# First four weight units converted during attention, and the odd groups' high part on GpSimd

## Chip, core and metric

The kernel runs on one core of a Trainium2 chip. The metric is the device time of one execution in microseconds, from the first to the last work of the core; lower is better.

## What is computed

An attention with head mixing (2 batches, 12 heads, 448 positions, head size 64) feeds two feed-forward blocks over 896 tokens of width 768. All inputs are float32 and the weights of the blocks are read as float64.

```python
scores = scale * q @ k.T                      # per head, then mixed over heads by w_pre
scores = scores - max(scores)
attn = exp(scores); attn = attn / (sum(attn) + 1e-9)
attn = mixed over heads by w_post;  x = attn @ v
xn = x / sqrt(mean(x*x) + 1e-6) * rms_g       # first block, width 1536
x = (silu(xn @ w_gate) * (xn @ w_val)) @ w_out
h = x @ w_in                                  # second block, width 2048
out = where(h > 0, h, exp(min(h, 0)) - 1) @ w_out2
```

## The kernel before

Products are made in split precision: each operand is a high part (float16 or a rounded float32) and a low part (the rest), and three matmuls add high x high, high x low, low x high (`gemm`, L202 to L204).

**Weights.** They come as *units* of 128 x 768 (one 768 KB load into a `raw` buffer, L208). A unit of the first block is *small* and is converted in eight stages: `rebase` (ScalarE L229, VectorE L232), `sign` (VectorE L237, L245), `join` (VectorE L251, for the second of a pair also L270), then once a pair `bound` (a TensorE matmul, L277) and `factor` (VectorE L284 to L290), then `scaled` (six ScalarE activations, L301), `high16` (ScalarE L305) and `low16` (VectorE L309). The result is a `whl` buffer, of which there are three. Units 0 and 2 are gate weights, 1 and 3 value weights of the same 128 columns.

**Attention.** It is cut into 90 groups (45 a batch) of 10 query positions x 12 heads = 120 rows. A hand-written loop over steps t = -6 to 94 records for each step one piece of the pipeline for several groups: the scores of a later group's rows come from `hq` (TensorE L469, copied by ScalarE L487, written to memory and read again as `sg`); the split of odd or even groups at t+3 (`g_split`: ScalarE L536, GpSimd L537, even groups alone); `g_premix` at t+1 (TensorE L544 for odd, *whole* groups, L547 to L549 for even ones); `g_max` at t (VectorE L556); `g_exp` at t (ScalarE L564); `g_sum` and `g_recip` at t-1 (VectorE L572, L579); `g_high` at t-1 (eh, VectorE L595, or ScalarE L593 for 20 of the 45 odd groups, in steps 20 to 43 and from 74); `g_low` at t-2 (el, VectorE L602); `g_postmix` at t-3 (TensorE L623, 12 matmuls); `g_out` at t-4 (ScalarE L635). Each engine does its instructions in the order in which they are recorded.

**Windows.** After every six or seven groups a window of tokens goes on: attention times v (TensorE L659), then a chain of stages, one a step: `squares` (VectorE L665, GpSimd L672 to L675 or, for the last two, ScalarE L670), `mean` (TensorE L681), `root` (VectorE L688, GpSimd L692: rstd), `diagonal` (VectorE L696: dg), `spread` (TensorE L702), `normed` (VectorE L705), `high` (ScalarE L711) and `low` (VectorE L714) of x. The first gate matmuls of the first block (`first_gate`) fill TensorE between these at the end; they need units 0 and 1, and from 292.58 us on the last window's x too.

**Where the conversions stand.** A list `tail` holds the pieces of units 0 and 1, one a step, which are begun when the list of scores `hq` is empty; a list `more` holds those of units 2 and 3, one for each piece of filling at the end. The high and low parts of q and k (`par`) live in nine rooms of their own and, the rest of them, in `whl` and `raw` buffers, which the weights can't use meanwhile.

Of the kernel before, what the change touches and what calls it, by code (L numbers as in the profile page):

```python
# [22 lines left out]
def block_kernel(  # L23
# [15 lines left out]
    nc = tc.nc  # L39
# [72 lines left out]
    g_top = const.tile([P, P], BF16, name="g_top")  # L112
    m1f = const.tile([GP, GP], F32, name="m1f")
    m1h = const.tile([GP, GP], F32R, name="m1h")
    m1l = const.tile([GP, GP], F32R, name="m1l")
    m2h = const.tile([GP, H, GI], F16, name="m2h")
# [9 lines left out]

    def mixing():

# [85 lines left out]
    def convert(u):  # L214
# [40 lines left out]
        def high():  # L255
            st["p"] = whl = wpool.tile([P, 2, n], F32R, tag="whl", name="whl", bufs=3)
            nc.scalar.activation(out=whl[:, 0], in_=st["w"], func=ACTF.Copy)  # L257
# [45 lines left out]
        def high16():  # L303
            st["p"] = whl = wpool.tile([P, 2, n], F16, tag="whl", name="whl16", bufs=3, padded_shape=[P, 4, n])
            nc.scalar.activation(out=whl[:, 0], in_=st["w"], func=ACTF.Copy)  # L305
# [64 lines left out]
    def attention(actx):  # L370
# [60 lines left out]
        def parts_of(b, p, tag):  # L431

            i = 2 * p + (tag == "qt")
            if (b, i) not in par:
                own = ["par"] * 9 + ["whl"] * 3 if b == 0 else ["raw"] * 2 + ["par"] * 9 + ["whl"]
                if own[i] == "par":
                    t = ap.tile([P, 2, S], F32R, tag="par", name="par", bufs=9)
                else:
                    n = 3 if own[i] == "whl" else 2
                    t = wpool.tile([P, 2 * KD * P], F32R, tag=own[i], name="par_" + own[i][0], bufs=n)  # L440
                    t = t[:, :2 * S].rearrange("p (t s) -> p t s", t=2)
                par[b, i] = t
            return [par[b, i][:, j] for j in range(2)]
# [137 lines left out]

        TURNS, LAST = range(20, 44), 74

        def high_on_act(b, g):
            i = b * NG + g
            return whole(b, g) and (i in TURNS or i >= LAST)

        def g_high(b, g):
            r = rows_of(g) * H
            e32, rs = ex[b, g]  # L590
            eh = ap.tile([GP, S], F16, tag="eh", name="eh", bufs=4)
            if high_on_act(b, g):
                nc.scalar.activation(out=eh[:r], in_=e32[:r], func=ACTF.Copy, scale=rs[:r])  # L593
            else:
                nc.vector.tensor_scalar_mul(eh[:r], e32[:r], rs[:r])  # L595
            ex[b, g].append(eh)
# [151 lines left out]
        MIX = 3  # L748
        mix = mixing()
        load_first()  # L750
# [48 lines left out]

        EARLY_GATES, GAP, FILL, END = 2, 2, 1, 1  # L800
        conv_now = []
# [15 lines left out]
        tail = [lambda: load_to(2)] + [lambda: None] * 2  # L817
        tail += unit() + [lambda: load_to(3)] + unit() + [lambda: load_to(4)] + scaling() + scaling()
        more = unit() + [lambda: load_to(5)] + unit() + [lambda: load_to(6)] + scaling()

        gates = []

        def fill(k):
            if not gates and not first_ps:
                while tail:
                    tail.pop(0)()
                for j in range(EARLY_GATES):
                    gates.extend(first_gate(j))
# [80 lines left out]
    def run(u, mm, stages):  # L909

        load_to(begun[0] + 2)
        v = begun[0]
        conv = []
        rest = next_scaled(u + 3 if u == 0 else u + 2)
        if v < len(units) and v <= u + (4 if units[v][4] else 2):
            conv = next_convert()
        conv = conv + [None] * (5 - len(conv))
        stages = stages + [None] * (4 - len(stages))

        def go(*fs):  # L920
# [13 lines left out]
        return out
# [190 lines left out]
```

## Time and profile before

| | before |
|---|---|
| median of 3 runs (us) | 782.35 (781.74 to 783.04) |
| profiled execution (us) | 782.59 |
| its span (us) | 780.9 |
| TensorE busy | 747.8 us, 96% |
| VectorE busy | 552.1 us, 71% |
| ScalarE busy | 438.5 us, 56% |
| GpSimd busy | 94.6 us, 12% |

The span runs from the first to the last instruction. A busy TensorE is one with a matmul under way, so holes are what is left of a stretch; TensorE's clock has two levels, 1.2 and 2.4 GHz, and a granted clock of 1.00 is the higher. Attention ends at about 293 us; the two blocks follow.

### The profile page before, as it was taken

How to read it: one execution, taken by the hardware profiler on the slowest of the kernel's cores; microseconds unless marked ns; L12 is line 12 of the kernel's file. 1: busy time of each engine (PE TensorE's matmuls, PEld its weight loads, DVE VectorE, ACT ScalarE, POOL GpSimd, SP SyncE). 2: the span in 40 equal slices, each digit the busy share in tenths (PEclk: the TensorE clock that was granted, in tenths of full speed). 3: DMA queues.
4: the chain of work that ended last, by engine and by line, in shares of the span. 5: the costliest groups of instructions: out<-in, count | busy, mean ns of one | idle time of the engine just before them, and what ended most of it. 6: DMA issues, size and time to landing. Idle time of an engine off the chain costs nothing.

```text
span 780.9 us, 14563 instructions
## 1 busy us (share of the span) xinstructions
PE 747.8 (96%) x5683; PEld 590.3 (76%) x5683; DVE 552.1 (71%) x1101; ACT 438.5 (56%) x910; POOL 94.6 (12%) x117
## 2 busy tenths in 40 slices
PE   7789999999998879999999999999999999999996
PEld 5446787777776654555555589999999999999996
DVE  4358997788899867878878766653888788643731
ACT  3478788878777845666576622322776665221310
POOL 0122344334445300000000000000000000000000
PEclk8689999999999999999999999999999999999999
DMA  8698965668675023333333223322444244442602
GB/s 186 202 298 263 188 142 147 186 177 251 188 200 156 3 84 122 99 112 114 122 122 119 83 83 122 122 81 72 131 122 119 87 119 120 124 121 79 174 22 71
DMA packets 92873, 104.05 MB, mean 133 GB/s; under 512 B 21316, under 2 KB 88708, under 8 KB 92804
## 3 DMA queue, kind: packets, MB, share of 16 engines
q1 hardware_dynamic: 92804, 103.12, 46.8%
q8 instruction: 45, 0.74, 0.4%
q14 instruction: 24, 0.20, 0.1%
HBM read 81.08 MB, written 22.02 MB: 132 GB/s over the span
## 4 chain that ended last, share of the span: by engine, by line
PE 82%; DVE 6%; DMA 5%; ACT 3%; SPq 2%; issue 1%; POOL 1%; ACTq 0%; POOLq 0%; DVEq 0%
PE psa_t L202 12%; PE psa_t L204 12%; PE psa_t L203 12%; PE psv_t L659 4%; PE pst_t L623 4%; PE psa_t L1081 4%; PE psa_t L1079 4%; PE psa_t L1080 4%; PE psf_t L204 3%; PE psf_t L202 3%; PE psf_t L203 3%; PE psa_t L544 3%; PE psa_t L469 3%; DMA s_d<-st 2%; PE psf_t L1079 1%; PE psf_t L1080 1%
## 5 line engine op out<-in xcount | busy, mean ns | idle before, releaser
L257 ACT ACTIVATE whl<-w 128x768 fp32r<-128x768 f32 x44 | 37.2, 846 | 100.0 <-DVE w L251 47.9
L623 PEld LDWEIGHTS <-eh 120*112 120x112 f16 x720 | 66.0, 130 | 24.4 <-issue 17.2
L261 DVE TENSOR_TENSOR whl<-w,whl 128x768 fp32r<-128x768 f32 x44 | 42.2, 958 | 59.5 <-ACT whl L257 59.5
L229 ACT ACTIVATE w<-raw 128x768 f32<-128x768 f32 x68 | 61.7, 907 | 20.9 <-DVE whl L309 18.9
L537 POOL TENSOR_TENSOR sl<-sg,sh 120x448 fp32r<-120x448 f32 (+1 forms) x45 | 57.0, 1266 | 115.2 <-ACT sh L536 112.5
L204 PE MATMUL psa_t<-x2h,whl 128*128 128x448 f32 x192 | 70.5, 367 | 0.0
L202 PE MATMUL psa_t<-x2h,whl 128*128 128x448 f32 x192 | 70.1, 365 | 0.0
L203 PE MATMUL psa_t<-x2l,whl 128*128 128x448 f32 x192 | 69.9, 364 | 0.0
L564 ACT ACTIVATE e<-psa_t,nmax 120x448 f32<-120x448 f32 (+1 forms) x90 | 57.4, 638 | 20.9 <-DVE rs L579 17.8
L623 PE MATMUL pst_t<-m2h,el 120*112 120x120 f16 x360 | 62.3, 217 | 5.6 <-DVE el L602 5.6
L251 DVE SCALAR_TENSOR_TENSOR w<-w,raw 128x768 int32<-128x768 int32 x68 | 65.2, 959 | 1.1
L602 DVE SCALAR_TENSOR_TENSOR el<-e,rs,eh 120x448 f16<-120x448 f32 (+1 forms) x90 | 65.6, 728 | 0.0
L245 DVE SCALAR_TENSOR_TENSOR raw<-raw 128x768 int32<-128x768 int32 x68 | 64.8, 953 | 0.0
L623 PE MATMUL pst_t<-m2h,eh 120*112 120x120 f16 x360 | 62.3, 216 | 0.2 <-DVE el L602 0.2
L623 PE MATMUL pst_t<-m2l,eh 120*112 120x120 f16 x360 | 62.3, 216 | 0.0
L556 DVE TENSOR_REDUCE nmax<-psa_t 120x1 f32<-120x448 f32 (+1 forms) x90 | 55.0, 611 | 9.1 <-PE psa_t L549 9.0
L301 ACT ACTIVATE w<-w,gs 128x128 f32<-128x128 f32 x144 | 44.5, 389 | 26.7 <-DVE gs L290 26.7
L202 PE MATMUL psa_t<-xhl,whl 128*128 128x448 f16 x150 | 53.6, 357 | 3.5 <-ACT xhl L711 3.5
L659 PE MATMUL psv_t<-at,vs 112*64 112x70 f32 (+3 forms) x1344 | 55.7, 230 | 0.3 <-DVE sm L572 0.3
L1080 PE MATMUL psa_t<-whl,gh 128*128 128x384 f32 x160 | 54.1, 338 | 0.0
L1081 PE MATMUL psa_t<-whl,gl 128*128 128x384 f32 x160 | 54.1, 338 | 0.0
L1079 PE MATMUL psa_t<-whl,gh 128*128 128x384 f32 x160 | 54.1, 338 | 0.0
(160 smaller groups left out, 1891.7 us busy)
## 6 DMA issues: line engine op xcount, KB each, us to landing
raw<-in_moe_w_out_dram SPq DMA_DIRECT2D x28, 768.0 KB, 4.5
sg<-s_d SPq DMA_DIRECT2D x44, 420.0 KB, 5.1
s_d<-st SPq DMA_DIRECT2D x93, 196.0 KB, 3.0
raw<-in_moe_w_in_dram SPq DMA_DIRECT2D x16, 768.0 KB, 4.7
raw<-in_moe_w_gate_dram SPq DMA_DIRECT2D x12, 768.0 KB, 4.4
raw<-in_moe_w_val_dram SPq DMA_DIRECT2D x12, 768.0 KB, 4.5
vs<-in_v_dram SPq DMA_DIRECT2D x12, 224.0 KB, 6.1
qk<-in_k_dram SPq DMA_DIRECT2D x6, 224.0 KB, 4.8
```

Of the source, the lines that this page charges most:

```text
L202: nc.tensor.matmul(out=ps, lhsT=wh(kk), rhs=xh_(kk), start=(first and kk == 0), stop=False)
L203: nc.tensor.matmul(out=ps, lhsT=wh(kk), rhs=xl_(kk), start=False, stop=False)
L204: nc.tensor.matmul(out=ps, lhsT=wl(kk), rhs=xh_(kk), start=False, stop=(last and kk == nk - 1))
L229: nc.scalar.activation(out=w, in_=raw.bitcast(F32)[:, :, 1], func=ACTF.Abs if small else ACTF.Copy, scale=REBASE)
L245: nc.vector.scalar_tensor_tensor(out=lo, in0=hi, scalar=SIGN, in1=lo, op0=ALU.bitwise_and, op1=ALU.bitwise_or)
L251: nc.vector.scalar_tensor_tensor(out=wi, in0=wi, scalar=3, in1=lo, op0=ALU.logical_shift_left, op1=ALU.bitwise_or)
L602: nc.vector.scalar_tensor_tensor(out=el[:r], in0=e32[:r], scalar=rs[:r], in1=eh[:r], op0=ALU.mult, op1=ALU.subtract)
L623: nc.tensor.matmul(out=o, lhsT=lhs[:r, c * CP:(c + 1) * CP], rhs=rhs[:r, :, :ni], start=(n == 0), stop=(n == 2),)
L659: nc.tensor.matmul(out=psx[s * D:(s + 1) * D, kk, :n], lhsT=vs[b, kk][:, s, c, :], rhs=at[:, c, hh, :n], start=(c == 0), stop=(c == NCH - 1),)
L1079: nc.tensor.matmul(out=o, lhsT=gh[:, kk, tk], rhs=wh[:, j], start=first, stop=False)
L1080: nc.tensor.matmul(out=o, lhsT=gh[:, kk, tk], rhs=wl[:, j], start=False, stop=False)
L1081: nc.tensor.matmul(out=o, lhsT=gl[:, kk, tk], rhs=wh[:, j], start=False, stop=end)
```

## The change

The parts of q and k get 12 rooms of their own, so `raw` and `whl` are free for weights during attention. `whl` has four buffers in place of three; m1f, m1h and m1l live in attention's pool. Units 0 to 3 are converted from one list of 43 pieces dealt over steps 28 to 84; `more` is gone, and the first run of the first block no longer scales a unit ahead by three. The high part of every odd group is made by GpSimd; that of even groups stays on VectorE.

```diff
-                own = ["par"] * 9 + ["whl"] * 3 if b == 0 else ["raw"] * 2 + ["par"] * 9 + ["whl"]
...
+                par[b, i] = ap.tile([P, 2, S], F32R, tag="par", name="par", bufs=2 * NP)
...
-            st["p"] = whl = wpool.tile([P, 2, n], F16, tag="whl", name="whl16", bufs=3, padded_shape=[P, 4, n])
+            st["p"] = whl = wpool.tile([P, 2, n], F16, tag="whl", name="whl16", bufs=4, padded_shape=[P, 4, n])
...
-        TURNS, LAST = range(20, 44), 74
-
-        def high_on_act(b, g):
-            i = b * NG + g
-            return whole(b, g) and (i in TURNS or i >= LAST)
-
...
-            if high_on_act(b, g):
-                nc.scalar.activation(out=eh[:r], in_=e32[:r], func=ACTF.Copy, scale=rs[:r])
+            if whole(b, g):
+                nc.gpsimd.tensor_scalar(out=eh[:r], in0=e32[:r], scalar1=rs[:r], scalar2=None, op0=ALU.mult)
             else:
                 nc.vector.tensor_scalar_mul(eh[:r], e32[:r], rs[:r])
...
-        EARLY_GATES, GAP, FILL, END = 2, 2, 1, 1
+        EARLY_GATES, UNITS, BEGIN, END_AT, GAP, FILL, END = 2, 4, 28, 84, 2, 1, 1
...
-        tail += unit() + [lambda: load_to(3)] + unit() + [lambda: load_to(4)] + scaling() + scaling()
-        more = unit() + [lambda: load_to(5)] + unit() + [lambda: load_to(6)] + scaling()
-
+        for j in range(0, UNITS, 2):
+            for i in range(2):
+                tail += unit() + [lambda n=j + i + 3: load_to(n)]
+            tail += scaling() + scaling()
+
+        pace = len(tail) / (END_AT - BEGIN)
...
-            if not hq and not on_act and not on_dve and tail:
-                tail.pop(0)()
+            for _ in range(int((t + 1 - BEGIN) * pace) - int((t - BEGIN) * pace) if t >= BEGIN else 0):
+                if tail:
+                    tail.pop(0)()
...
-        rest = next_scaled(u + 3 if u == 0 else u + 2)
+        rest = next_scaled(u + 2)
```

The end of attention, on VectorE, where the last window's x is made: w_ are the weights in conversion, inv, up and gs the factors of a pair. Line numbers of the kernel after lie a few lines lower. Before:

```order
L251 SCALAR_TENSOR_TENSOR w_4979<-w_4979,raw 128x768
L270 TENSOR_SCALAR wm<-wm 128x2
L705 TENSOR_TENSOR xt<-xt,psw_t 128x6x60
L688 TENSOR_SCALAR ms<-psw_t 48x1
L284 TENSOR_SCALAR inv<-psa_t 128x2
L288 RECIPROCAL up<-inv 128x2
L290 TENSOR_TENSOR gs<-g_dn,up 128x12
L714 TENSOR_TENSOR xhl<-xt,xhl 128x6x60
L696 TENSOR_SCALAR dg<-ident,rstd 48x48
L309 TENSOR_TENSOR whl_5066<-w_4858,whl_5066 128x768
L705 TENSOR_TENSOR xt<-xt,psw_t 128x6x48
L714 TENSOR_TENSOR xhl<-xt,xhl 128x6x48
```

and after:

```order
L680 TENSOR_SCALAR dg<-ident,rstd 60x60
L649 TENSOR_TENSOR xt<-psv_t,vsc 128x6x48
L689 TENSOR_TENSOR xt<-xt,psw_t 128x6x60
L672 TENSOR_SCALAR ms<-psw_t 48x1
L698 TENSOR_TENSOR xhl<-xt,xhl 128x6x60
L680 TENSOR_SCALAR dg<-ident,rstd 48x48
L689 TENSOR_TENSOR xt<-xt,psw_t 128x6x48
L698 TENSOR_TENSOR xhl<-xt,xhl 128x6x48
```

The conversion pieces of units 2 and 3 (L251, L270, L284 to L290, L309) no longer stand between the last windows' stages.

The same place on ScalarE (sq are the squares, xhl the high part of x, at the exit of a group's postmix). Before:

```order
L229 ACTIVATE w_4979<-raw 128x768
L711 ACTIVATE xhl<-xt 128x6x60
L670 ACTIVATE sq<-xt 128x6x48
L711 ACTIVATE xhl<-xt 128x6x60
L301 ACTIVATE w_4858<-w_4858,gs 128x128 x6
L305 ACTIVATE whl_5066<-w_4858 128x768
L711 ACTIVATE xhl<-xt 128x6x48
L229 ACTIVATE w_5089<-raw 128x768
L301 ACTIVATE w_4979<-w_4979,gs 128x128 x6
```

and after:

```order
L654 ACTIVATE sq<-xt 128x6x60
L619 ACTIVATE at<-pst_t 112x48x8
L695 ACTIVATE xhl<-xt 128x6x60
L654 ACTIVATE sq<-xt 128x6x48
L695 ACTIVATE xhl<-xt 128x6x60
L695 ACTIVATE xhl<-xt 128x6x48
L226 ACTIVATE w_5098<-raw 128x768
L226 ACTIVATE w_5125<-raw 128x768
```

Scaling and high parts of the weights no longer stand in front of the last xhl; the next unit's rebase (L226 of after) follows it.

In the middle of attention, on VectorE, around step 41: sm, nmax, rs, el and eh are one group's steps, dg and xt a window's. Before:

```order
L556 TENSOR_REDUCE nmax<-psa_t 120x1
L579 RECIPROCAL rs<-sm 120x1
L602 SCALAR_TENSOR_TENSOR el<-e_2392,rs,eh 120x448
L665 TENSOR_TENSOR xt<-psv_t,vsc 128x6x60
L572 TENSOR_SCALAR sm<-sm 120x1
L556 TENSOR_REDUCE nmax<-psa_t 120x1
L579 RECIPROCAL rs<-sm 120x1
L602 SCALAR_TENSOR_TENSOR el<-e_2436,rs,eh 120x448
L595 TENSOR_SCALAR eh<-e_2474,rs 120x448
L705 TENSOR_TENSOR xt<-xt,psa_t 128x6x60
```

and after:

```order
L546 TENSOR_REDUCE nmax<-psa_t 120x1
L569 RECIPROCAL rs<-sm 120x1
L586 SCALAR_TENSOR_TENSOR el<-e_2407,rs,eh 120x448
L234 TENSOR_SCALAR w_2465,wm<-w_2465 128x768
L242 SCALAR_TENSOR_TENSOR raw<-raw 128x768
L649 TENSOR_TENSOR xt<-psv_t,vsc 128x6x60
L562 TENSOR_SCALAR sm<-sm 120x1
L546 TENSOR_REDUCE nmax<-psa_t 120x1
L569 RECIPROCAL rs<-sm 120x1
L586 SCALAR_TENSOR_TENSOR el<-e_2449,rs,eh 120x448
L579 TENSOR_SCALAR eh<-e_2492,rs 120x448
L248 SCALAR_TENSOR_TENSOR w_2465<-w_2465,raw 128x768
```

The sign and join steps of unit 1 (L234, L242, L248 of after) now stand between two groups' el there.

On GpSimd, somewhat earlier, around a window's squares. Before:

```order
L675 TENSOR_TENSOR sq<-sq 128x70
L537 TENSOR_TENSOR sl<-sg,sh 120x448
L692 TENSOR_TENSOR rstd<-ms,mhalf 70x1
L537 TENSOR_TENSOR sl<-sg,sh 120x448 x2
L672 TENSOR_TENSOR sq<-xt 128x420
```

and after:

```order
L659 TENSOR_TENSOR sq<-sq 128x70
L577 TENSOR_SCALAR eh<-e_1514,rs 120x448
L527 TENSOR_TENSOR sl<-sg,sh 120x448
L577 TENSOR_SCALAR eh<-e_1609,rs 120x448
L676 TENSOR_TENSOR rstd<-ms,mhalf 70x1
L527 TENSOR_TENSOR sl<-sg,sh 120x448
L577 TENSOR_SCALAR eh<-e_1712,rs 120x448
```

An eh (L577 of after) for every odd group now stands among the low parts sl, behind a window's squares or its rstd.

## Rows read from the trace of the kernel before

**Rows 1.** Busy us (instructions) of each engine by stage, granted clock, DMA share, GB/s.

```profile
0.00:88.00 88.00, 73.76 (x591) 51.54 (x592) 51.86 (x138) 53.94 (x123) 17.55 (x25) 0.86 0.85 232
88.00:148.00 60.00, 59.56 (x798) 47.70 (x797) 51.48 (x140) 49.95 (x120) 23.22 (x29) 1.00 0.71 159
148.00:225.00 77.00, 76.39 (x1002) 59.10 (x1000) 66.40 (x173) 60.73 (x149) 32.39 (x40) 1.00 0.70 193
225.00:264.00 39.00, 34.70 (x457) 27.43 (x454) 36.80 (x92) 28.00 (x67) 17.38 (x17) 0.96 0.53 145
264.00:293.00 29.00, 21.44 (x325) 15.46 (x324) 20.44 (x50) 16.43 (x38) 4.05 (x7) 0.94 0.18 57
293.00:773.00 480.00, 480.00 (x2509) 387.47 (x2508) 323.96 (x512) 228.99 (x418) 0.00 (x0) 1.00 0.35 106
```

**Rows 2.** Shorter stretches: the first three of TensorE alone, the last of all engines.

```profile
230.00:237.00 7.00, 4.11 (x44) 1.00 0.89 210
237.00:242.00 5.00, 4.12 (x43) 0.66 0.68 211
242.00:264.00 22.00, 21.47 (x307) 1.00 0.27 72
...
293.00:297.00 4.00, 4.00 (x14) 1.67 (x13) 3.19 (x6) 2.07 (x7) 0.00 (x0) 0.61 0.00 0
```

**Rows 3.** TensorE in order of time: start, duration, [idle before, releaser], four of its holes.

```profile
236.07 0.26 PE L623 MATMUL pst_t<-m2h,el 120*112 120x120 f16 x1 [2.70 <-DVE el L602]
...
272.92 0.26 PE L623 MATMUL pst_t<-m2h,el 120*112 120x120 f16 x1 [1.10 <-DVE el L602]
...
288.67 0.39 PE L702 MATMUL psw_t<-dg,ones 48*128 48x48 f32 x2 [1.37 <-DVE dg L696]
...
292.58 0.53 PE L202 MATMUL psa_t<-xhl,whl 128*128 128x448 f16 x1 [3.52 <-ACT xhl L711]
```

**Rows 4.** VectorE in order of time, ahead of the hole at 236 us.

```profile
231.67 0.94 DVE L237 TENSOR_SCALAR_CACHE_REDUCE w<-w 128x768 f32<-128x768 f32 x1
...
235.16 0.86 DVE L602 SCALAR_TENSOR_TENSOR el<-e,rs,eh 120x448 f16<-120x448 f32 x1
```

**Rows 5.** All engines in order of time, ahead of the last two holes.

```profile
286.09 0.15 DVE L688 TENSOR_SCALAR ms<-psw_t 48x1 f32<-48x1 f32 x1 [0.49 <-PE psw_t L681]
...
286.32 0.54 POOL L692 TENSOR_TENSOR rstd<-ms,mhalf 48x1 f32<-48x1 f32 x1 [6.33 <-DVE ms L688]
...
288.29 0.23 DVE L696 TENSOR_SCALAR dg<-ident,rstd 48x48 f32<-48x48 f32 x1
...
290.73 0.96 DVE L309 TENSOR_TENSOR whl<-w,whl 128x768 f16<-128x768 f32 x1 [2.21 <-ACT whl L305]
291.61 0.45 DVE L705 TENSOR_TENSOR xt<-xt,psw_t 128x288 f32<-128x288 f32 x1
292.09 0.44 ACT L711 ACTIVATE xhl<-xt 128x288 f16<-128x288 f32 x1 [1.39 <-DVE xt L705]
```

**Rows 6.** Groups by line, whole span: busy us, mean ns of one, idle before, releasers.

```profile
L251 DVE SCALAR_TENSOR_TENSOR w<-w,raw 128x768 int32<-128x768 int32 x68 | 65.2, 959 | 1.1
...
L245 DVE SCALAR_TENSOR_TENSOR raw<-raw 128x768 int32<-128x768 int32 x68 | 64.8, 953 | 0.0
...
L232 DVE TENSOR_SCALAR raw<-raw 128x768 int32<-128x768 int32 x68 | 37.7, 555 | 0.7 <-DMA raw<-in_moe_w_gate_dram 0.7
...
L309 DVE TENSOR_TENSOR whl<-w,whl 128x768 f16<-128x768 f32 x24 | 22.9, 956 | 8.5 <-ACT whl L305 8.1
L237 DVE TENSOR_SCALAR_CACHE_REDUCE w<-w 128x768 f32<-128x768 f32 x24 | 22.8, 949 | 8.9 <-ACT w L229 8.9
```

**Rows 7.** Groups by line on VectorE from 148 to 225 us.

```profile
L595 DVE TENSOR_SCALAR eh<-e,rs 120x448 f16<-120x448 f32 (+1 forms) x29 | 19.3, 665 | 0.0
```

**Rows 8.** Groups by line: GpSimd, whole span, and TensorE, 88 to 264 us.

```profile
L537 POOL TENSOR_TENSOR sl<-sg,sh 120x448 fp32r<-120x448 f32 x44 | 55.8, 1268 | 113.3 <-ACT sh L536 110.6 <-PE pst_t L623 2.7
...
L544 PE MATMUL psa_t<-sg,m1f 120*120 120x448 f32 (+1 forms) x70 | 35.9, 595 | 0.1
```

**Rows 9.** SyncE's queue, who waited for whom: us, times, longest.

```profile
SPq L508 <- PE psa_t L544: 31.2, 13, 4.9
```

**Rows 10.** VectorE and GpSimd in order of time, one eh beside one sl.

```profile
238.42 1.32 DVE L595 TENSOR_SCALAR eh<-e,rs 120x448 f16<-120x448 f32 x1
...
237.99 1.51 POOL L537 TENSOR_TENSOR sl<-sg,sh 120x448 fp32r<-120x448 f32 x1 [0.16 <-ACT sh L536]
```

More of the change, by code (lines that the diff above doesn't have):

```diff
@@ L112, in block_kernel @@
     g_top = const.tile([P, P], BF16, name="g_top")
-    m1f = const.tile([GP, GP], F32, name="m1f")
-    m1h = const.tile([GP, GP], F32R, name="m1h")
-    m1l = const.tile([GP, GP], F32R, name="m1l")
     m2h = const.tile([GP, H, GI], F16, name="m2h")
@@ L125, in load_small, with mixing @@
         )
-    def mixing():
+    def mixing(m1f, m1h, m1l):
         selr, cmax, rcm, m2p = slot(H, GI, H), slot(P, H), slot(P, H), slot(GP, H, GI)
@@ L255, in high @@
         def high():
-            st["p"] = whl = wpool.tile([P, 2, n], F32R, tag="whl", name="whl", bufs=3)
+            st["p"] = whl = wpool.tile([P, 2, n], F32R, tag="whl", name="whl", bufs=4)
             nc.scalar.activation(out=whl[:, 0], in_=st["w"], func=ACTF.Copy)
@@ L434, in parts_of @@
             if (b, i) not in par:
-                own = ["par"] * 9 + ["whl"] * 3 if b == 0 else ["raw"] * 2 + ["par"] * 9 + ["whl"]
[L436 to L442, printed above, removed]
+                par[b, i] = ap.tile([P, 2, S], F32R, tag="par", name="par", bufs=2 * NP)
             return [par[b, i][:, j] for j in range(2)]
@@ L748, in attention @@
         MIX = 3
-        mix = mixing()
+        m1f = ap.tile([GP, GP], F32, tag="m1f", name="m1f", bufs=1)
+        m1h = ap.tile([GP, GP], F32R, tag="m1h", name="m1h", bufs=1)
+        m1l = ap.tile([GP, GP], F32R, tag="m1l", name="m1l", bufs=1)
+        mix = mixing(m1f, m1h, m1l)
         load_first()
@@ L830, in fill @@
                 gates.pop(0)()
-            if more:
-                more.pop(0)()
         for t in range(-6, n + 5):
@@ L849, in attention @@
             at_step(g_low, t - 2)
-            if not (0 <= t - 1 < n and high_on_act(*seq[t - 1])):
-                at_step(g_high, t - 1)
+            at_step(g_high, t - 1)
             follow(on_dve)
@@ L856, in attention @@
             at_step(g_exp, t)
-            if 0 <= t - 1 < n and high_on_act(*seq[t - 1]):
-                at_step(g_high, t - 1)
             at_step(g_postmix, t - 3)
@@ L895, in attention @@
         fill(len(gates))
-        while more:
-            more.pop(0)()
     with ExitStack() as actx:
```

## The prediction, made before the changed kernel ran

> **What bounds the kernel now.** I first read the busy time by stage [rows 1]. From 293 to 773 us TensorE is busy 480.00 of 480.00 us at full clock: the two feed-forward blocks are a matmul stream without a hole, and nothing that other engines give up can shorten it. From 88 to 225 us, the middle of attention, TensorE lacks only 0.44 and 0.61 us, though VectorE is at 51.48 of 60 and 66.40 of 77 us. So there is something to win in three places alone: the start (88 minus 73.76, 14.2 us idle), the late steps of attention (225 to 264 us, 4.3 us idle) and its end (264 to 293 us, 7.6 us idle). Every matmul is the same before and after the change; the sum can only move TensorE's holes.
>
> The second reading is the clock. After the holes the granted clock is 0.66 from 237 to 242 us and 0.61 from 293 to 297 us [rows 2]: the lower level, half of 2.4 GHz, for part of each stretch, after an engine that had just stood. That costs 4.12 busy us x 0.34 = 1.4 us and 4.00 x 0.39 = 1.6 us more. All there is to win late and at the end is 4.3 + 7.6 + 1.4 + 1.6 = 14.9 us.
>
> The third is who ends the holes [rows 3]. At 236 us the postmix matmul waits 2.70 us for el on VectorE, at 273 us 1.10 us for the same, at 288.7 us 1.37 us for dg on VectorE, and at 292.6 us 3.52 us for the last high part of x on ScalarE. VectorE's own rows say why el is late at 236 us [rows 4]: two steps of a weight unit's conversion (L237 at 231.67, L245 behind it) stand between one group's el and the next, which starts only at 235.16. The last hole is the same thing in a row [rows 5]: dg starts at 288.29 although the rstd that it needs is there at 286.86, and L705, which the last high part needs, stands behind a conversion's L309 at 290.73, which itself waits 2.21 us for ScalarE's scaling and high part. So conversions that stand among the last steps make nearly all of the late holes.
>
> **The change part by part.** *Conversions.* A small unit costs VectorE 0.555 + 0.949 + 0.953 + 0.959 + 0.956 = 4.37 us [rows 6], of which 3.42 come in its first three stages. Before, units 0 and 1 do those at 229 to 250 us and their rest at 263 to 272, units 2 and 3 all of it behind 272 us. After, the 43 pieces are dealt over steps 28 to 84, about three in four steps: heavy stages near steps 34 to 37, 40 to 43, 59 to 63 and 66 to 69, and the last low part before step 84, so nothing of it is left for the last six groups. Taken from 225 to 293 us: 3 units' and a half of VectorE work, and the waits that came with it.
>
> What that gives: at 225 to 264 us TensorE has 39 - 4.3 - 1.4 = 33.3 us of work, and VectorE 36.80 - 2 x 3.42 + 2 x 0.956 = 31.9 us. That fits, but tightly, so I leave 0.8 us of holes. At the end I walk the chain again from the same durations [rows 5]: ms at 286.09, rstd 286.32 to 286.86, dg from 286.95 in place of 288.29, its matmul 0.15 us behind it (0.39 us), L705 0.45 us, L711 0.44 us: the first gate matmul could start at 288.7 in place of 292.58, 3.85 us earlier. Of 1.37 + 3.52 = 4.9 us, 1.0 stays; with the low part, which the second matmul needs, I leave 1.5. With holes that short the drop of the clock at 293 us should go too: the 1.10 us hole at 273 us is followed by none. Won: 14.9 - 0.8 - 1.5 = 12.6 us.
>
> What it costs in the middle: between 88 and 148 us two units' first stages add 6.8 us to VectorE's 51.48, 58.3 of 60; there the odd groups' high parts were on ScalarE, so VectorE gets nothing back. Between 148 and 225 us, 2 x 3.42 + 2 x 0.956 = 8.7 us are added and 14 or 15 of the 29 L595 at 0.665 us leave [rows 7], 9.7 us: no change at 66 of 77 us. The hole that a unit can tear is bounded by none (the middle's idle is 0.61 us with VectorE as full) and by what the first unit tore at 230 to 242 us (7.00 + 5.00 minus busy 4.11 + 4.12, and the clock, 5.2 us [rows 2]), four times: 20.7 us. I take 2.0 us in all, near the lower end: at 230 us a piece came in every step and TensorE's steps were at their shortest, here three pieces come in four steps and the scores lengthen TensorE's steps. ScalarE loses the high parts and takes about as much scaling; it is at 50 of 60 and 61 of 77 us [rows 1] and hides that.
>
> *The high part on GpSimd.* 45 instructions leave VectorE (25) and ScalarE (20) for GpSimd. No row shows this operation there. The nearest is the same size with two inputs, 1.27 us mean [rows 8]; the other end is VectorE's own 0.665. I take 1.0 us; an end above is 3.0, since nothing in the rows excludes a slow scalar form. 35 of these groups lie between 88 and 264 us (70 rows of L544, two a group [rows 8]), where GpSimd is busy 23.22 + 32.39 + 17.38 = 73.0 of 176 us [rows 1]. With 35 us more it is at 61%: covered. Who waits for it is VectorE's el, one step later, about 2.4 us, and GpSimd's squares and rstd in front of it move it within that step. If that cover is gone, el is late and TensorE's postmix with it, as at 236 us. I book nothing.
>
> *The rooms.* 12 rooms for the parts of q and k in place of borrowed weight rooms, a fourth whl, m1 moved: no instruction more, and the loads of raw can go out at step 28. They pass SyncE's queue in front of sg loads, which wait for buffers anyway (31.2 us for the premix that frees them [rows 9]); cost nothing, bounds 0 and 2 us, in the 2.0 above. At the start VectorE loses ten high parts, but TensorE's holes there lie before 70 us, where scores make their round through memory: nothing booked, 1.5 us either way.
>
> Sum against the profiled execution (782.59 us, span 780.9): 12.6 - 2.0 = 10.6 us, 772.0; it lies 0.24 above the median, so 771.8.
>
> **A rule against the change.** VectorE's eh took 1.32 us at 238.42, when GpSimd's sl ran from 237.99 to 239.50 [rows 10], against a mean of 0.665: it ended 0.24 us behind GpSimd's end. So GpSimd's time is not free for VectorE. The Trainium skill says why (SBUF — State Buffer, Who interferes with whom): the two share a pair of ports, which one instruction holds for all its time while the other blocks; this pair of rows agrees. By that rule each new GpSimd instruction can hold back VectorE, which is rival B. A page on the price: the Trainium skill (GPSIMD Engine Reference, Engine selection) sends elementwise work to VectorE and counts one-input forms near line rate; by that the price would lie below my 1.0 us, and the sum would be the same.
>
> **The rivals.** A: the middle has room and the late steps too; holes of 1.5 us stay and no new ones come, and the start gains 1.5: 782.35 - 14.9 + 1.5 - 1.5 = 767.5. For it, the idle 0.6 us beside a full VectorE. B: the held ports. If each of the 35 middle instructions holds VectorE for 0.4 us more, VectorE needs 58.3 + 12 x 0.4 = 63.1 of 60 us in the first stretch and 31.9 + 8 x 0.4 = 35.1 of 33.3 in the late one: 3.1 + 1.8 us more holes less the 0.8 counted, 771.8 + 4.1 = 775.9. Against it: the new instruction starts behind rs, when VectorE turns to el and then to sum and maximum, and not to another high part. C, the slower side: each unit's burst tears the hole that the first tore before, 5.2 us, in the middle: 782.35 - 12.6 + 20.7 = 790.5; it decides from 12.6/4 = 3.2 us a unit. Against it: the second unit before, at 243 to 250 us, tore next to nothing (242 to 264 us: TensorE 21.47 of 22.00 [rows 2]). D: GpSimd is the bound. It fills at (176 - 73)/35 = 2.9 us an instruction and eats the gain at 2.9 + 10.6/35 = 3.2 us; at 3.5 us it is slower, 771.8 + 0.6 x 35 = 793. E: the holes come back where they were, because the last groups' exponentials, now over GpSimd, end no earlier: 782.
>
> **How the numbers follow.** Forecast 0.50, A 0.18, B 0.16, C 0.06, D 0.05, E 0.05. Range 765.5 (A with a better start) to 779.0 (B with another 3 us of holes). Faster by over 0.2% (1.6 us, about what a measurement can tell): forecast, A and B, 0.84; within it: 0.05; slower: C and D, 0.11.
>
> **What would show it.** Right: TensorE's idle at 225 to 264 falls below 1.5 us, no wait for L711 above 1.5 us at the end, no clock below full at either place, and the middle's idle below 3 us. Wrong, step by step: holes that wait for el near the four bursts (C); L602, or the conversion rows, longer beside GpSimd (B); the new GpSimd rows at 2.9 us or more (D); the same holes at the end with other releasers (E).

## The result and the profile after

The changed kernel is slower: 792.45 us median (791.70 to 794.04) against 782.33 (781.74 to 783.04) before, a ratio of 1.0132 with an interval of 1.0114 to 1.0149. That is 10 us the wrong way, 20.7 us above the forecast and outside the range.

The stages of the profiled execution (792.33 us, span 790.6), to be read against [rows 1] and [rows 2]:

```profile
88.00:148.00 60.00, 56.15 (x762) 44.71 (x761) 54.86 (x132) 43.45 (x105) 42.03 (x38) 1.00 0.74 174
148.00:225.00 77.00, 69.91 (x899) 53.51 (x898) 64.00 (x161) 58.20 (x145) 53.50 (x49) 1.00 0.76 209
225.00:264.00 39.00, 34.92 (x424) 26.71 (x424) 34.65 (x81) 25.61 (x65) 25.04 (x24) 0.96 0.53 141
264.00:293.00 29.00, 26.44 (x396) 20.90 (x394) 23.66 (x57) 17.82 (x44) 19.48 (x19) 1.00 0.01 2
293.00:310.00 17.00, 15.62 (x178) 9.72 (x178) 9.68 (x21) 3.51 (x6) 1.31 (x2) 1.00 0.06 17
310.00:773.00 463.00, 463.00 (x2422) 372.40 (x2421) 316.88 (x499) 224.43 (x407) 0.00 (x0) 1.00 0.36 109
```

The middle, which had 0.44 and 0.61 us of holes on TensorE, now has 3.85 and 7.09. VectorE is a little fuller in the first stretch (54.86 of 60 us in place of 51.48) and less full in the second (64.00 of 77 in place of 66.40). GpSimd is much fuller, at 42.03 and 53.50 us in place of 23.22 and 32.39, but has time left as well. So TensorE isn't waiting for an engine without time, but for one that is late.

The end did what was forecast. The last wait before the first feed-forward block, 3.52 us in [rows 3], is now 1.02 us, and the granted clock that fell to 0.61 there in [rows 2] is 1.00 from 293 to 310 us. (From 225 to 264 us it is 0.96, as before.) ScalarE and TensorE in order of time:

```profile
303.44 0.44 ACT L695 ACTIVATE xhl<-xt 128x288 f16<-128x288 f32 x1 [2.57 <-DVE xt L689]
...
303.93 0.35 PE L199 MATMUL psa_t<-xhl,whl 128*128 128x448 f16 x1 [1.02 <-ACT xhl L695]
```

But it stands at 303.93 us in place of 292.58. The groups of the whole span (busy us, mean ns, idle before and its releasers) show the new instruction and its reader el, which in the kernel before was the first row here:

```profile
L602 DVE SCALAR_TENSOR_TENSOR el<-e,rs,eh 120x448 f16<-120x448 f32 (+1 forms) x90 | 65.6, 728 | 0.0
```

```profile
L586 DVE SCALAR_TENSOR_TENSOR el<-e,rs,eh 120x448 f16<-120x448 f32 (+1 forms) x90 | 79.8, 886 | 15.4 <-POOL eh L577 15.0
...
L577 POOL TENSOR_SCALAR eh<-e,rs 120x448 f16<-120x448 f32 (+1 forms) x45 | 75.7, 1683 | 40.7 <-DVE rs L569 32.4
```

GpSimd's eh takes 1.68 us in the mean, not 1.0, and VectorE now stands still for it for 15.0 us in front of el; el itself is longer, 0.89 us in place of 0.73. The waits from 88 to 264 us (us in all, times, longest), one of before and three of after, show who is behind that:

```profile
ACT e L564 <- DVE rs L579: 16.4, 17, 2.8
```

```profile
ACT e L554 <- DVE rs L569: 37.7, 25, 3.8
...
DVE el L586 <- POOL eh L577: 11.9, 17, 2.0
...
PE pst_t L607 <- DVE el L586: 4.3, 7, 1.0
```

The wait that one would look for, TensorE's postmix for el, is only 4.3 us. The larger one is ScalarE's exponential, which waits for VectorE's rs of the group before: 37.7 us in place of 16.4. How one becomes the other is to be read in the chain of waits, here one piece of it (start, length, what):

```profile
210.46 0.51 DVE xt L649
...
211.05 0.90 POOL sq L656
...
212.01 0.82 POOL sq L657
...
212.91 0.31 POOL sq L658
...
213.30 0.13 POOL sq L659
...
213.61 1.42 POOL eh L577
...
215.05 1.55 DVE el L586
216.59 0.36 DVE eh L579
216.96 0.86 DVE w L248
...
218.32 0.53 DVE nmax L546
218.85 0.08 DVE rs L569
```

and in ScalarE's and TensorE's own rows behind it:

```profile
218.94 0.64 ACT L554 ACTIVATE e<-psa_t,nmax 120x448 f32<-120x448 f32 x1 [3.30 <-DVE rs L569]
...
219.72 0.46 PE L537 MATMUL psa_t<-sh,m1h 120*120 120x448 f32 x1 [0.91 <-ACT e L554]
```

A window's squares take GpSimd for 2.6 us, eh stands behind them, and VectorE had been ready for el at 213.2 us and starts it at 215.05. VectorE does its instructions in order: behind el stand an eh, a conversion step, the next sum, maximum and reciprocal, so everything that the next group needs is 1.9 us later. The exponential waits for that rs, the premix for the exponential. Most of the loss never shows as a wait for eh on TensorE.

The wait has a second price. GpSimd goes on to its next instruction when eh ends, the moment at which el starts:

```profile
214.98 1.13 POOL L527 TENSOR_TENSOR sl<-sg,sh 120x448 fp32r<-120x448 f32 x1
```

```profile
215.05 1.55 DVE L586 SCALAR_TENSOR_TENSOR el<-e,rs,eh 120x448 f16<-120x448 f32 x1 [1.88 <-POOL eh L577]
```

This el takes 1.55 us, where one beside which GpSimd is idle takes 0.68, and ends 0.48 us after the sl. Twelve el of this trace start within 0.07 us of an sl's start. All el together take 79.8 us in place of 65.6.

In the whole chain that ended last GpSimd's share goes from 1% (the first line, of before) to 6% (after):

```profile
PE 82%; DVE 6%; DMA 5%; ACT 3%; SPq 2%; issue 1%; POOL 1%; ACTq 0%; POOLq 0%; DVEq 0%
```

```profile
PE 73%; DVE 9%; DMA 6%; POOL 6%; ACT 2%; issue 2%; SPq 1%; POOLq 0%; ACTq 0%; DVEq 0%
```

### The profile page after: what moved, and what is told of

The parts are those of the page before. It is cut to its first block, busy times and chain, and to the rows that moved or that the text cites. A ratio compares the mean times of both kernels' runs of the same rounds, so it can differ in the third digit from the quotient of the medians.

```text
span 790.6 us, 14586 instructions
## 1 busy us (share of the span) xinstructions
PE 755.0 (95%) x5683; PEld 592.7 (75%) x5683; DVE 553.3 (70%) x1076; ACT 426.5 (54%) x890; POOL 171.0 (22%) x162
## 4 chain that ended last, share of the span: by engine, by line
PE 73%; DVE 9%; DMA 6%; POOL 6%; ACT 2%; issue 2%; SPq 1%; POOLq 0%; ACTq 0%; DVEq 0%
PE psa_t L200 12%; PE psa_t L201 12%; PE psa_t L199 12%; POOL eh L577 4%; PE psa_t L1064 3%; PE psa_t L1065 3%; PE psa_t L1063 3%; PE psf_t L201 3%; PE psf_t L199 3%; PE psf_t L200 3%; DVE el L586 3%; DMA s_d<-st 3%; PE pst_t L607 3%; PE psv_t L643 2%; PE psa_t L534 2%
## 5 line engine op out<-in xcount | busy, mean ns | idle before, releaser
L586 DVE SCALAR_TENSOR_TENSOR el<-e,rs,eh 120x448 f16<-120x448 f32 (+1 forms) x90 | 79.8, 886 | 15.4 <-POOL eh L577 15.0
L577 POOL TENSOR_SCALAR eh<-e,rs 120x448 f16<-120x448 f32 (+1 forms) x45 | 75.7, 1683 | 40.7 <-DVE rs L569 32.4
L554 ACT ACTIVATE e<-psa_t,nmax 120x448 f32<-120x448 f32 (+1 forms) x90 | 57.8, 642 | 44.3 <-DVE rs L569 44.1
L226 ACT ACTIVATE w<-raw 128x768 f32<-128x768 f32 x68 | 61.6, 908 | 25.4 <-DVE whl L306 18.9
L248 DVE SCALAR_TENSOR_TENSOR w<-w,raw 128x768 int32<-128x768 int32 x68 | 65.2, 959 | 1.1
L242 DVE SCALAR_TENSOR_TENSOR raw<-raw 128x768 int32<-128x768 int32 x68 | 65.4, 962 | 0.0
L527 POOL TENSOR_TENSOR sl<-sg,sh 120x448 fp32r<-120x448 f32 (+1 forms) x45 | 55.3, 1230 | 43.1 <-ACT sh L526 42.2
L619 ACT ACTIVATE at<-pst_t 112x480 f32<-112x480 f32 (+1 forms) x90 | 52.4, 582 | 3.7 <-PE pst_t L607 3.4
L1063 PE MATMUL psa_t<-whl,gh 128*128 128x384 f32 x160 | 53.4, 334 | 0.0
```

What stands on the lines that cost most here:

```text
L226: nc.scalar.activation(out=w, in_=raw.bitcast(F32)[:, :, 1], func=ACTF.Abs if small else ACTF.Copy, scale=REBASE)
L242: nc.vector.scalar_tensor_tensor(out=lo, in0=hi, scalar=SIGN, in1=lo, op0=ALU.bitwise_and, op1=ALU.bitwise_or)
L248: nc.vector.scalar_tensor_tensor(out=wi, in0=wi, scalar=3, in1=lo, op0=ALU.logical_shift_left, op1=ALU.bitwise_or)
L554: nc.scalar.activation(out=e32[:r], in_=ps[:r, :S], func=ACTF.Exp, bias=nmax[:r], scale=1.0, accum_out=sm[:r])
L577: nc.gpsimd.tensor_scalar(out=eh[:r], in0=e32[:r], scalar1=rs[:r], scalar2=None, op0=ALU.mult)
L586: nc.vector.scalar_tensor_tensor(out=el[:r], in0=e32[:r], scalar=rs[:r], in1=eh[:r], op0=ALU.mult, op1=ALU.subtract)
```

## The experiments

Three explanations for the 20.7 us above the forecast: the lateness just read (GpSimd's eh ends too late for el; L in the expectations); the load that the new instructions put on GpSimd and, by held ports, on VectorE, whoever waits (P); and the bursts of conversions in the middle (rival C).

### One part of the change at a time

**e1**, the changed kernel with the high parts back where they were:

```diff
...
-            if whole(b, g):
-                nc.gpsimd.tensor_scalar(out=eh[:r], in0=e32[:r], scalar1=rs[:r], scalar2=None, op0=ALU.mult)
+            if high_on_act(b, g):
+                nc.scalar.activation(out=eh[:r], in_=e32[:r], func=ACTF.Copy, scale=rs[:r])
...
```

> The changed kernel with one of its two parts undone: the conversions stay at steps 28 to 84, the odd groups' high parts go back to VectorE and (20 of them) ScalarE. Theory L (lateness: GpSimd's eh, 1.68 us, comes too late for el) and theory P (ports: GpSimd's added 76 us hold VectorE up) both say that the loss leaves with GpSimd: 768 to 774 us, the gain of about 10 that the prediction gave to the conversions. Theory C (the conversion pieces tear the holes in the middle): 788 us or more.

**e2**, the kernel before with the odd groups' high parts on GpSimd, and nothing else:

```diff
-            if high_on_act(b, g):
-                nc.scalar.activation(out=eh[:r], in_=e32[:r], func=ACTF.Copy, scale=rs[:r])
+            if whole(b, g):
+                nc.gpsimd.tensor_scalar(out=eh[:r], in0=e32[:r], scalar1=rs[:r], scalar2=None, op0=ALU.mult)
...
```

> The kernel before with the other part alone: all 45 odd groups' high parts on GpSimd, conversions where they were. L and P: slower than before by the 18 us that attention lost up to step 89 in the changed kernel, so 795 to 803 us. C: within 2 us of 782.

Measured: e1 773.17 us (768.59 to 775.19), ratio to before 0.9884 (0.9842 to 0.9927); e2 794.24 us (793.53 to 795.16), ratio 1.0163 (1.0137 to 1.0188), just under the 795 to 803 expected. The conversions gain 9 us; the high part costs 12 us in the old kernel and 792.45 - 773.17 = 19.3 us in the new one. Rival C is out: with all four bursts in the middle e1 is the faster kernel. Its stages from 148 us on (its profile is from an execution of 768.6 us, its shortest):

```profile
148.00:225.00 77.00, 72.74 (x915) 55.25 (x910) 69.06 (x179) 62.11 (x154) 34.28 (x38) 1.00 0.73 206
225.00:264.00 39.00, 37.24 (x527) 29.78 (x526) 36.77 (x101) 32.77 (x83) 16.66 (x19) 1.00 0.38 93
264.00:283.00 19.00, 18.65 (x304) 13.80 (x303) 8.57 (x25) 6.50 (x14) 4.04 (x7) 1.00 0.01 3
```

and, from 88 to 264 us, the wait that stood at 37.7 us:

```profile
ACT e L554 <- DVE rs L569: 17.4, 18, 2.6
```

In e2 the long eh is there, and with it el's wait (75 to 305 us), without any conversion moved:

```profile
L593 POOL TENSOR_SCALAR eh<-e,rs 120x448 f16<-120x448 f32 (+1 forms) x45 | 75.5, 1678 | 40.1 <-DVE rs L579 27.6 <-PE psa_t L469 3.2 <-PE psa_t L549 2.7
```

```profile
DVE el L602 <- POOL eh L593: 10.8, 17, 1.9
```

Where each loses is told by when TensorE starts the first premix matmul of a group (us, in the profiled execution of each):

| premix of group | before | after | e1 | e2 |
|---|---|---|---|---|
| 28 | 106.9 | 108.9 | 104.0 | 107.5 |
| 44 | 147.5 | 155.1 | 145.0 | 151.3 |
| 74 | 225.0 | 240.8 | 228.1 | 231.4 |
| 89, the last | 263.4 | 281.0 | 261.7 | 272.9 |
| end of the span | 780.9 | 790.6 | 766.9 | 792.4 |

### Load or lateness

**e3**, e1 with 45 instructions on GpSimd whose result nobody reads: all of the load, and no el that waits for it (against e1).

```diff
+            if whole(b, g):
+                junk = ap.tile([GP, NCH, CP], F16, tag="junk", name="junk", bufs=1)
+                nc.gpsimd.tensor_scalar(
+                    out=junk[:r], in0=ones[:r, :CP].unsqueeze(1).to_broadcast([r, NCH, CP]), scalar1=rs[:r],
+                    scalar2=None, op0=ALU.mult,
+                )
```

> e1_high_back with 45 GpSimd instructions added that nobody waits for: the same form and size as eh, behind the same rs, from a constant into a scratch tile. GpSimd is as busy as in the changed kernel, but no el needs it. L: within 3 us of e1_high_back. P: most of the way back to the changed kernel, 783 to 792 us.

**e4**, the changed kernel with one more step between eh and el: all of the load, and time to wait.

```diff
-            at_step(g_low, t - 2)
+            at_step(g_low, t - 3)
...
-            at_step(g_out, t - 4)
+            at_step(g_out, t - 5)
...
-            at_step(g_postmix, t - 3)
+            at_step(g_postmix, t - 4)
```

(and a buffer more for e32, rs and eh, one less for xt).

> The changed kernel with one step more between eh and el (el three steps behind the exponential, postmix four, exit five; one buffer more for e32, rs and eh, one less for xt). GpSimd does the same work. L: el no longer waits for eh, most of the holes in the middle close, 774 to 780 us. P: GpSimd holds VectorE as before, 788 to 794 us.

Measured: e3 779.32 us (777.03 to 785.36), ratio 0.9969 (0.9944 to 0.9994); e4 780.00 us (778.00 to 787.37), ratio 0.9994 (0.9968 to 1.0019). Neither explanation holds alone: e3 lies between what L (within 3 us of e1) and P (783 or more) gave, and e4 at the end of L's 774 to 780. The two come to the same place from opposite sides. Load without waiting costs 779.3 - 773.2 = 6.2 us over e1; taking the waiting away gives 792.45 - 780.0 = 12.4 us. Together they are 18.6 of the 19.3; the interval of e1 alone leaves some 3 us on either side, so that the sum is as close as this is partly luck. e4's eh is no shorter, it only has time (group of eh, then VectorE's wait for it, 14.8 us in the same stretch, 75 to 305 us, of after):

```profile
L577 POOL TENSOR_SCALAR eh<-e,rs 120x448 f16<-120x448 f32 (+1 forms) x45 | 81.6, 1812 | 23.3 <-DVE rs L569 15.1 <-PE psa_t L459 2.2 <-PE psa_t L538 2.0
```

```profile
DVE el L586 <- POOL eh L577: 3.5, 5, 1.6
```

### What makes eh late: its length or its place

**e5** prices the operation: the 45 idle instructions of e3 in five forms.

```diff
+                if k == 0:
+                    nc.gpsimd.tensor_scalar(out=junk[:r], in0=src, scalar1=rs[:r], scalar2=None, op0=ALU.mult)
+                elif k == 1:
+                    nc.gpsimd.tensor_scalar(out=junk[:r], in0=src, scalar1=2.0, scalar2=None, op0=ALU.mult)
+                elif k == 2:
+                    nc.gpsimd.tensor_tensor(out=junk[:r], in0=src, in1=src, op=ALU.mult)
+                elif k == 3:
+                    nc.gpsimd.tensor_copy(out=junk[:r], in_=src)
...
```

> The kernel of e1 with an instruction on GpSimd for each of the 45 odd groups whose result nobody reads: nine each of five forms, all reading the same float32 constant and writing float16. k=0: 120x448, multiplied by a scalar of its own for each partition (the form of eh); k=1: 120x448 times one constant; k=2: 120x448, product of two tensors; k=3: 120x448, a plain copy; k=4: as k=0 with half the elements. It prices the operation by itself. Theory S (a one-input instruction with a scalar is slow on GpSimd as such): shortest k=0 about 1.4 to 1.6 us, k=4 half of it plus 0.1, k=2 about 1.1, as sl. Theory F (the float16 output makes it slow): k=0 to k=3 all about 1.4 to 1.6. Theory W (the 1.68 us mean of eh is mostly waiting for VectorE): all forms of 448 elements have shortest times near 1.1 and means above 1.5. Time about 778 us, between e1 (773.2) and e3 (779.3).

Groups on GpSimd (busy us, mean ns, idle before):

```profile
L586 POOL TENSOR_SCALAR junk<-ones,rs 120x448 f16<-120x448 f32 x9 | 16.3, 1813 | 4.2 <-DVE rs L569 4.2
L588 POOL TENSOR_SCALAR junk<-ones 120x448 f16<-120x448 f32 x9 | 14.3, 1592 | 0.0
L594 POOL TENSOR_SCALAR junk<-ones,rs 120x224 f16<-120x224 f32 x8 | 10.7, 1342 | 3.4 <-DVE rs L569 3.1 <-PE psa_t L687 0.3
L590 POOL TENSOR_TENSOR junk<-ones 120x448 f16<-120x448 f32 x9 | 10.1, 1128 | 0.0
L592 POOL CAST junk<-ones 120x448 f16<-120x448 f32 x9 | 7.4, 827 | 0.1
```

The shortest of each was 1.60, 1.33, 0.87, 0.92 and 0.69 us. They are not quite like for like: the forms with rs mostly start behind idle time of GpSimd, the other three right behind another instruction, and in after the shortest eh takes 1.65 us behind idle time and 1.40 right behind another instruction. Among the 45 of e3, which have the form of k=0, the shortest is 1.41 us. Even against that the product of two tensors is shorter than the product with a scalar, and a plain copy with the same float16 output is the shortest: theories F and W fall, and S holds (k=4 at 0.87 us is half of 1.60 plus 0.1), but for k=2, which is shorter than its 1.1. The one execution took 782.88 us, within the spread of e3; nothing follows from that time.

**e6**, the changed kernel with only those eh back on VectorE that stand right behind a window's squares:

```diff
-            if whole(b, g):
+            behind = bool(held)
+            held.clear()
+            if whole(b, g) and not behind:
...
+                held.append(w)
                 nc.gpsimd.tensor_tensor(out=sq[:, :, :n], in0=xt[:, :, :n], in1=xt[:, :, :n], op=ALU.mult)
```

> The changed kernel, but the high part of an odd group whose place in GpSimd's queue is right behind a window's squares goes back to VectorE (some 8 of the 45); all else as in the changed kernel. In its trace nine such groups made VectorE's el wait 6.5 of 15.0 us. Theory Q (the lateness is the queue: eh stands behind the squares): about half of the 12.4 us that one more step gave comes back, 786 us (785 to 787.5). Theory D (the lateness is the instruction's own 1.4 to 1.7 us against one step, wherever it stands): 8 of 45 of 12.4 us, 2.2 us, 790. Theory P (load and held ports): 8 of 45 of 6.2, 1.1 us, 791.

Measured: 785.82 us (782.53 to 790.01), ratio 1.0043 (1.0022 to 1.0065); 6.6 us less than after. The expectation miscounted what moves: most have an sl between the squares and eh, and only the three right behind the squares went to VectorE (42 of 45 stay). In after these three made el wait longest, two of them here in VectorE's order of time, the third is the one at 215.05 us above:

```profile
106.03 1.55 DVE L586 SCALAR_TENSOR_TENSOR el<-e,rs,eh 120x448 f16<-120x448 f32 x1 [1.42 <-POOL eh L577]
...
254.24 1.54 DVE L586 SCALAR_TENSOR_TENSOR el<-e,rs,eh 120x448 f16<-120x448 f32 x1 [1.97 <-POOL eh L577]
```

That is 1.42 + 1.88 + 1.97 = 5.3 us for three instructions, and the time fell by 6.6: nearly us for us, theory Q's time. In e6, from 75 to 305 us, what is left is many short waits:

```profile
DVE el L590 <- POOL eh L581: 9.0, 19, 1.3
```

In five of these 19 (3.2 of the 9.0 us) eh stood right behind an sl or a window's rstd. In the other 14 (5.9 us) GpSimd had been idle and began eh when rs came, so that nothing but eh's own length makes el wait. After has 14 such waits too, this one among them (rs is there at 218.92 us, VectorE ready for el at 220.46):

```profile
219.12 1.66 POOL L577 TENSOR_SCALAR eh<-e,rs 120x448 f16<-120x448 f32 x1 [3.00 <-DVE rs L569]
```

```profile
220.81 0.69 DVE L586 SCALAR_TENSOR_TENSOR el<-e,rs,eh 120x448 f16<-120x448 f32 x1 [0.35 <-POOL eh L577]
```

So three places in GpSimd's queue make about half of the lateness; most of the rest is, by the waits, eh's own length.

**e8**, the changed kernel with the same product written with two tensors:

```diff
-                nc.gpsimd.tensor_scalar(out=eh[:r], in0=e32[:r], scalar1=rs[:r], scalar2=None, op0=ALU.mult)
+                nc.gpsimd.tensor_tensor(out=eh[:r], in0=e32[:r], in1=rs[:r].to_broadcast([r, S]), op=ALU.mult)
```

> The changed kernel, with GpSimd's high part written as a product of two tensors (the second the reciprocal, repeated along the row) in place of a multiplication by a scalar; the same numbers come out. In the traces the two-input sl of the same size takes 1.13 us at the shortest, the one-input eh 1.40. Theory D (the instruction's own length makes el late): eh 0.27 us shorter, the 23 waits of el shrink by about 6 us, 786 to 788 us. Theory Q or P (its place in the queue, the ports): 791 to 793. If the form with a repeated operand is no faster, eh stays at 1.4 us and the time at 792.4.

Measured: 779.79 us (777.83 to 783.84), ratio 0.9969 (0.9949 to 0.9988): 12.7 us less than after, twice what theory D gave. The two groups, el's idle time for eh among them:

```profile
L586 DVE SCALAR_TENSOR_TENSOR el<-e,rs,eh 120x448 f16<-120x448 f32 (+1 forms) x90 | 69.0, 767 | 5.6 <-POOL eh L577 5.6
...
L577 POOL TENSOR_TENSOR eh<-e,rs 120x448 f16<-120x448 f32 (+1 forms) x45 | 54.2, 1205 | 34.9 <-DVE rs L569 25.8 <-PE psa_t L459 2.9 <-PE psa_t L686 1.7
```

The form saves 0.48 us an instruction, not the 0.27 that I took from the shortest ones, and el beside it falls from 0.89 to 0.77 us. Behind idle time eh now takes 1.20 us in place of 1.66, which fits into the 1.5 us between rs and el in the rows above.

**e9**, both cures (e8 and the further step of e4) in one kernel:

> The changed kernel with both cures: GpSimd's high part as a product of two tensors (e8) and one more step between it and el (e4). Alone, the first gave 12.7 us (792.45 to 779.8) and the second 12.4 us (to 780.0). Theory S (both take away the same lateness of el, and what remains above e1's 773.2 is GpSimd's load and the held ports): 778 us (776.5 to 780), no sum. Theory A (two different losses, which add up): 767 to 770. In e8 el still waited 5.6 us in 7 cases; if each of these still costs TensorE its time: 774 to 775.

Measured: 779.79 us (778.22 to 782.01), ratio 0.9972 (0.9953 to 0.9992). No sum: el's wait falls from 5.6 to

```profile
DVE el L586 <- POOL eh L577: 1.1, 1, 1.1
```

and the time stays, as theory S gave it. Both cures took the same 12.6 us, and the 6.6 us above e1 are not waiting for eh.

### What the load costs, and a better version

**e7**, e1 with each window's mean, and the stages behind it, one step further behind GpSimd's squares:

```diff
-            chain = [squares, None, mean, root, None, diagonal, spread, normed, high, low]
+            chain = [squares, *[None] * (1 if late else 2), mean, root, None, diagonal, spread, normed, high, low]
```

> The kernel of e1 (conversions moved, high parts as before the change) with each window's mean on TensorE one step later behind GpSimd's squares, except for the last two windows, whose squares are ScalarE's. In e1 TensorE's holes in attention that end with the squares (at 199.9 us 1.86, 236.5 us 1.87, 218.7 us 1.54 and smaller ones) make 5 to 6 us. If the sequence only waits for those squares: 769 us (767 to 771). If what is behind in the stream is late by itself (el, exponentials), the holes get other releasers and the time stays at 773 (772 to 774). Slower, 774 or more, if a window's bank of sums held one step longer delays the scores that need one.

**e10**, e3's idle instructions in e7:

> The kernel of e3 (e1 with 45 instructions on GpSimd whose result nobody reads) with the later mean of e7. It splits the 6.2 us that those instructions cost (773.2 to 779.3). Theory Q (they delay what else is in GpSimd's queue, above all the squares that the mean waits for: 4.6 us of holes in e3's trace): with the later mean that is hidden, and the time is within 2 us of e7, 771 to 773. Theory P (they hold VectorE's instructions, 7 us more in all for eh and el in the trace of e3 than in e1's): the cost stays, 770.7 plus 6, 776.5 to 778.

Measured: e7 770.74 us (769.63 to 772.00), ratio 0.9849 (0.9824 to 0.9874); e10 774.64 us (773.29 to 778.20), ratio 0.9909 (0.9876 to 0.9941). e7 beats both kernels and has the lowest median of all; that it beats e1 is not shown, since their intervals overlap, and with that the expectation's choice stays open. The 5 to 6 us of holes that it reads from e1 (1.86 us at 199.9 us) don't stand in e1's trace. TensorE's waits for the squares, 1.3 us in e1's table of waits, are gone, and others are there instead (75 to 285 us):

```profile
PE psa_t L537 <- ACT e L554: 2.3, 2, 1.4
PE psa_t L459 <- ACT e L554: 1.1, 1, 1.1
PE psa_t L440 <- DVE rs L569: 1.1, 1, 1.1
```

Over 0.4 us each, its holes from 75 to 290 us still add up to 6.9 us, as in e1 (6.8). The price of the idle instructions fell from 6.2 us (e3 over e1) to 3.9 (e10 over e7): between what theories Q and P gave. That squares delayed behind them were about a third of it is likely by e3's row, against those 1.3 us in e1,

```profile
PE psa_t L677 <- POOL sq L671: 4.6, 5, 2.2
```

but the spreads of these kernels don't settle how much. For the other two thirds e3's groups on VectorE speak: eh (x70) and el (x90) together take 44.3 + 69.3 us against 40.6 + 65.9 in e1, 7.1 us more:

```profile
L598 DVE SCALAR_TENSOR_TENSOR el<-e,rs,eh 120x448 f16<-120x448 f32 (+1 forms) x90 | 69.3, 770 | 0.2 <-ACT eh L589 0.2
L591 DVE TENSOR_SCALAR eh<-e,rs 120x448 f16<-120x448 f32 (+1 forms) x70 | 44.3, 634 | 0.0
```

But it is mostly not the idle instructions that lengthen them. Of the 29 eh of VectorE in e3 that start beside an idle instruction 24 take 0.44 us, as alone; of the eight that start beside an sl seven take 1.32 us or more. Of the 43 eh and el that take longer than alone, 37 end 0.25 us (eh) or 0.48 us (el) after the end of an sl or of one of a window's squares. In after all 48 do. What the new instructions change, then, is how often VectorE meets the two-input instructions that stood on GpSimd before; how the last 6 us come about is not settled.

## Why the prediction was wrong

**The reading of what bounds it was right.** The feed-forward blocks kept their full TensorE, the last hole at the end shrank from 3.52 to 1.02 us and the clock's drop at 293 us went, both as forecast. In the late steps (225 to 264 us) the granted clock stayed at 0.96 in the changed kernel; in e1 it is 1.00.

**The conversions were right in sum, in part by luck.** They were booked at -12.6 + 2.0 = -10.6 us, to 771.8. e1, which is that part alone, has 773.17. By the table of groups its profiled execution won 17.1 us from group 74 to the end (780.9 - 225.0 against 766.9 - 228.1), lost 6.0 us between groups 28 and 74, where I booked 2.0, and won 2.9 us before, where I booked nothing. The 17.1 us are more than the 14.9 that I called all there is to win there; where the rest comes from is open. That execution is 4.6 us below e1's median, so the sizes hold for it alone, but the terms' errors are of opposite sign and nearly cancel, and that is luck. The middle's idle from 148 to 225 us alone is 4.26 us in e1, where I had set 3 as the bound for the whole middle; from 225 to 264 us it is 1.76, where I had set 1.5.

**The step that failed is the high part on GpSimd, "I book nothing".** It costs 19.3 us. Three things are in it.

First its price. I took 1.0 us, between VectorE's 0.665 and the two-input 1.27 of [rows 8]: one input less, so shorter. It is 1.40 us at the shortest, 1.66 where GpSimd was idle before it, and 1.68 in the mean. The end of 3.0 that I kept for the range wasn't used: I asked only when GpSimd would be full (2.9 us) and not when eh would be late.

Second, and that is the larger error, the cover. I added up GpSimd's busy time (61% with the new work, "covered"), but what el needs is not GpSimd's time over 176 us, it is this one eh before VectorE turns to el. I took one step of about 2.4 us for that; in the trace of after it is 1.8 us in the median, from the end of rs, and 1.5 in many steps, so that eh is late there even with nothing in front of it. I named the squares and rstd in front of it and said they move it "within that step", without adding: squares 2.6 us and eh 1.41 make 4.0 us, as the piece of the chain at 211 us shows. Both numbers could be had from before: the squares' rows, and 1.0 to 3.0 for eh. Even my own 1.0 would have made 3.6 of 2.4 us. By e6 three such places cost 6.6 us, half of the lateness; by e4, e8 and e9 this lateness is 12.4 to 12.7 us, about two thirds of the loss.

Third, what waits. I wrote that el would be late "and TensorE's postmix with it". The postmix waits 4.3 us. The rest goes through VectorE's order: el stands in front of the next group's sum, maximum and reciprocal, and the exponential's wait for rs grew from 17.4 us in e1 to 37.7; el itself, started beside the next sl, takes longer.

**The rivals.** B, the held ports, came near in size, not in mechanism: what remains when nothing waits (6.2 us, e3 over e1; 6.6, e8 and e9 over e1) is above its price of 4.1 us. I let each new instruction hold VectorE for 0.4 us; e3's 7.1 us of longer VectorE instructions make 0.16 for each of the 45, and they were mostly held by sl and the squares, which were there before; squares held up on GpSimd come beside it. My argument against it, that VectorE turns to el and not to a high part, was wrong: el is held too (0.73 us in e1, 0.77 beside e3's idle instructions, 0.89 in after). C fell with e1. D named the right engine with the wrong test, full instead of late: GpSimd has 17.97 of 60 and 23.50 of 77 us left in the middle. The slower side got 0.11, on C and D alone; the mechanism that decided wasn't among the rivals, though the sentence that names it stood in the part on costs.

That the high part costs 12 us in e2 and 19.3 us in the changed kernel is not settled by a run. By the table of groups, in which the two differ by 11.5 and 23.7 us, it costs more in the new kernel before group 28 (0.6 us in the old kernel, 4.9 in the new), from 28 to 44 (3.2 and 5.2), from 74 to 89 (3.1 and 6.6) and behind the last premix (2.0 and 4.4). In the last two the conversions' leaving had shortened the steps, so that the same eh has less time; that is a reading, not a result, and for the first two there is none.

## What to carry to other kernels

Work moved to an engine with time to spare must be priced at the place where its reader stands: add what is queued in front of it and its own length, and compare with the distance to the reader, not with the engine's busy share. Then ask what stands behind the reader in its engine's order, since the loss shows there under another name. And where a change has two parts, give each its own sign: here one alone gained 9 us, and the other cost 12 alone and 19 on top of it.

## What the hardware showed that was not expected

**On GpSimd a product with a scalar takes longer than a product of two tensors.** 120x448 from float32 to float16 took, at the shortest, 0.69 us as a copy, 0.92 as a product of two tensors and 1.33 as a product with a constant (e5), and 1.41 with a scalar for each partition (e3), all reading one constant; on the exponentials themselves 0.92 with two tensors (e8) and 1.40 with a scalar (after). The Trainium skill (GPSIMD Engine Reference, Engine selection) counts one-input forms near line rate and two-input ones slower. Here that order doesn't hold for the products: the two-input form is the shorter by a third.

**VectorE's length depends on what GpSimd does beside it.** In the trace of after, counted by overlap and in the mean, VectorE's eh takes 0.44 us alone and 0.79 beside a GpSimd instruction, el 0.68 and 0.92, and the maximum over 448 elements 0.61 and 0.61. For el that agrees with the Trainium skill (SBUF — State Buffer, Who interferes with whom), which says that a VectorE instruction with two SBUF inputs contends with a GpSimd instruction that reads SBUF; the maximum reads PSUM here, so it tests nothing. The mean hides that a few instructions are held for most of a microsecond and the others hardly: by its median (0.68 us) el beside a GpSimd instruction is as short as alone, and every longer one ends right behind an sl or a window's squares. Beside GpSimd's one-input eh, which reads SBUF too, the 21 el of e4 that start there take 0.66 to 0.70 us; nearly all of them start late in it, so that this is no test. In e8 el beside a GpSimd instruction takes 0.79 in place of 0.92.
